# Twenty-five instead of fourteen seven-product pairs in a fused attention and mixer kernel, with a new order of all its tasks

## The chip, the cores and the metric

The kernel runs on one core of one Trainium2 chip. A core has five engines that work side by side, each through its own instructions in a fixed order: PE (TensorE, matrix products, into the eight banks of PSUM), DVE (VectorE), ACT (ScalarE), POOL (GpSimd, here almost only an issuer of DMAs) and SP (SyncE, an issuer of DMAs). They wait for each other by semaphores. The metric is the device time of one execution in microseconds (us); the time of a kernel is the median of its runs.

## The reference

Windowed attention with a distance bias, then a low-rank mixer over the sequence and an MLP with a residual:

```python
B, H, S, D = q.shape                      # 4, 8, 768, 64
scores = scale * np.matmul(q, k.transpose(0, 1, 3, 2))
# keep: the first 8 keys, and the 96 keys up to the query; bias: -slope[h] * distance
a = np.exp(scores - scores.max(-1)) / (sum + 1e-09)
x = (a @ v).transpose(0, 2, 1, 3).reshape(B, S, 512)
xt = x.transpose(0, 2, 1)
h = xt @ U @ V                            # U: 768 x 32, V: 32 x 768
u = x + h.transpose(0, 2, 1)
out = u + np.maximum(u @ w_ch1, 0.0) @ w_ch2   # w_ch1: 512 x 2048, w_ch2: 2048 x 512
```

## The kernel before

**Tasks and their order.** The kernel describes its work as some hundreds of tasks, each with a name, an engine, a function that issues its instructions, the tasks it needs, and the buffers it takes and gives back (`Task`, `Group`, `Planner`). A planner that ran earlier has fixed everything that can vary: `ORDER` is the list of all tasks in issue order, `SLOTS` the buffer or PSUM bank of each group, `CFG` which engine does a task that several could do. `Planner.run` checks that list against the needs, and a loop at the end issues the tasks as listed, so each engine's order is that of `ORDER`.

**The stages, by name.** A number behind the name is the pair (0 to 15: two heads of one batch, four pairs a batch) or batch and part.

- Loads: `lq`, `lk`, `lv` (q, k, v of a pair; POOL, but for pair 0, whose q and k come as fp32 on SP and are cast by `Cq`, `Ck`), `w1_0` to `w1_7` and `w2_0` to `w2_3` (slices of the MLP weights, POOL), `u16` (U), `mixl`, `vs` (V of the mixer).
- Constants: `iota`, `relf`, `rel3` (distances), `bias` (scaled identities in `ib`), `mask` (exponentials of the distances, ACT).
- Attention of a pair: `TK`, `TQ` (transposes on PE for the early pairs, by DMA on SP from pair 8), `EK`, `EQ` (their copies out of PSUM), `KO` and `VC`/`VG` (copies of K and V with the global keys at the front of each block), `SB` (bias by PE, batch 0), `S` (scores), `EX` (exponential, ACT), `MK` (multiplication by the mask, DVE, batches 1 to 3), `PV` (values), `RC`, `NM` (division, DVE), `XC` (copy to fp16).
- Mixer: `UP` transposes x by PE and multiplies it by U. Every pair multiplies with U at 32 columns (`xu` is true, line 752), so that the result lies with tokens on partitions' side; then `XE` copies it out four times over (128 columns), `XU` turns it by one more matmul (line 855), `TE` copies that out as `tmp`, `HM` multiplies by V and adds it to the transposed x, `E0`/`E1` copy the sum out as `uT`, the input of the MLP.
- MLP-1 (u @ w_ch1, 16 column blocks of 128, two halves of the tokens): a plain block is `M1a`.. `M1b` (four matmuls of 384 columns for each half; lines 927 and 951) and a ReLU on ACT (`RL`, `RM`).
- Blocks z and z+8 can be done as a pair with seven products instead of eight (`Z` in `CFG`, line 1022 and after): `ZT` forms four differences of `uT` once a batch, `ZS` four sums of weights, kept in `zs` or formed anew in an `ep` buffer, `ZP1` to `ZP7` are two matmuls of 384 columns each into three PSUM banks, `ZU`, `ZW`, `ZX` copy partial sums to fp32 buffers (ACT, four buffers `zu` in batches 0 to 2), `ZA`, `ZB`, `ZD` add them with the ReLU (a custom DVE instruction, line 1040), `ZR` is the fourth ReLU (ACT). Before, 14 of the 32 pairs are done so: z = 4 to 7 in batches 1 and 2, 2 to 7 in batch 3.
- MLP-2 (h @ w_ch2): always seven products, `P1` to `P7` of eight matmuls of 256 columns each (line 1139), with sums of its operands by DVE (`PA`, `PB`, lines 1092 to 1098; `TWa`, `TWb` once for the weights), a low-rank part by `RS`, additions to the residual by `DA`, `DB`, `DC`, `DD`, `DF`, `DG`, `DH` (lines 1151 and 1191) and stores `O` on SP (line 1206). In the last batch the third part of the tokens is cut into halves (`P43.2a`, `P43.2b`, `DG3.2a`, `DG3.2b`, stores `a`, `b`, `c`).

**What stands around.** MLP-1 and MLP-2 of a batch are interleaved with the attention of the next. Ahead of the first transpose eight matmuls of 512 columns on zeros run (`WARM`, `idle`, line 1240); nothing reads their result.

Of the kernel before, what the change touches and what calls it, by code (L numbers as in the profile page):

```python
# [26 lines left out]
TK5 TE0 RC2 HM0 NM2 lk7 PV3.0 E00 TK4 PV3.1 EK5 XC2 UP1 RC3.0 RC3.1 TQ5 EK4 w1_5 XE1 PV3.2 EQ5 XU1 UP2 NH3.0 w1_6 TQ4
NH3.1 XE2 TE1 RC3.2 XU2 EQ4 lv4 HM1 TE2 NH3.2 HM2 E01 KO4 back UP3.0 mixl w1_2 UP3.1 UP3.2 NM3 M1a0.3 XE3 lv5 E02 XU3
M1c0.3 TE3 mask2 HM3 w1_4 S4.1 E13 E03 M1d0.3 KO5 EX4.1 w1_0 TK7 M1b0.15 EK7 M1a0.2 vs2 lq6 RM0.15 M1b0.3 KO7 EX4.2
M1a0.15 M1c0.2 RL0.3 M1a0.13 RL0.15 S4.0 S5.0 EX4.0 M1d0.2 lq7 M1b0.13 RL0.13 M1b0.11 EX5.0 M1b0.2 mask1 w1_3 M1a0.4  # L30
RL0.2 M1a0.10 w2_2 mask0 RL0.4 S5.1 MK4.2 RM0.13 w2_0 M1a0.12 MK4.1 RM0.11 EX5.2 M1a0.14 VC4 ZS5 M1b0.14 RL0.10 VG4
RL0.14 M1b0.10 VC5 mask5 MK4.0 M1a0.11 EX5.1 lk6 M1a0.0 mask3 M1c0.0 PV4 RM0.10 MK5.2 w2_3 RL0.11 TQ7 RM0.14 RC4
M1b0.5 VG5 RL0.12 w2_1 NM4 M1b0.4 lv7 MK5.1 XC4 M1b0.8 PA0.3 M1d0.0 RM0.8 M1b0.0 M1b0.6 TD0 RL0.0 lq9 MK5.0 M1a0.7
RM0.4 RM0.6 PV5 M1b0.12 RC5 EQ7 M1a0.5 NM5 RM0.12 RM0.5 M1b0.7 RL0.5 TWa0 M1a0.6 RL0.7 mask6 lk9 TK6 RM0.7 M1a0.1
TWb0 EK6 M1c0.1 M1b0.9 M1d0.1 PB0.3 RM0.9 M1b0.1 RL0.6 TQ6 lq8 RL0.1 UP4 EQ6 M1a0.9 KO6 XE4 PA0.0 XU4 M1a0.8 TE4
RL0.9 PA0.1 RS0.0 RL0.8 S7.0 lv8 HM4 P10.0 E04 PA0.2 EX7.0 P20.0 lv6 PB0.0 XC5 S6.1 RS0.1 PB0.1 EX6.2 lk8 P10.1 PB0.2
EX6.1 P20.1 lk11 TWa1 UP5 P30.0 XE5 mask4 TQ8 TWb1 P50.0 lv9 XU5 P30.1 TE5 DA0.0 MK6.1 S6.0 HM5 DA0.1 EX6.0 P60.0
DF0.0 E05 VC6 P60.1 DF0.1 MK6.2 S7.1 TK8 VC7 RS0.2 VG6 EX7.1 P10.2 DB0.1 MK7.0 TK9 EX7.2 P50.1 MK6.0 VG7 MK7.1 P70.1
TQ9 MK7.2 P30.2 VC8 ZS7 PV6 KO8 lk10 DB0.0 PV7 DC0.0 P20.2 DD0.1 DA0.2 lq10 RC7 P70.0 RC6 NM7 P40.1 NM6 XC7 lk12
P60.2 DG0.1 XC6 DF0.2 UP7 KO9 DD0.0 lq11 UP6 DB0.2 XE7 DC0.1 P40.0 XE6 TK10 XU6 XU7 P70.2 lv11 DG0.0 TE6 TE7 VC9 TQ10  # L40
HM6 lv10 HM7 DD0.2 S8.0 E17 ZP11.4 E07 EX8.0 P40.2 ZS4 lq13 E06 S8.1 P50.2 ZT1 EX8.1 ZP11.5 EX8.2 M1a1.3 ZU1.5 lk13
M1b1.3 ZU1.4 ZP61.5 RL1.3 ZP21.5 VG11 ZP61.4 ZA1.5 ZW1.5 S9.1 ZW1.4 DC0.2 M1b1.6 EX9.1 O0.1 ZS6 ZP71.5 ZP71.4 MK8.2
O0.4 ZX1.5 lq12 ZP11.7 EX9.2 O0.2 M1a1.7 DG0.2 TQ11 ZP51.4 RL1.7 ZP41.5 RM1.6 ZP21.4 ZP51.5 ZR1.5 O0.0 M1a1.6 ZB1.5
M1a1.2 ZA1.4 ZX1.4 O0.3 MK9.1 RL1.6 O0.5 ZP21.7 TK11 ZB1.4 M1b1.2 MK8.1 ZP41.4 M1a1.5 VG8 ZR1.4 MK8.0 ZU1.7 ZP31.4
ZP11.6 RL1.2 KO10 ZD1.4 ZP31.5 ZP61.7 ZA1.7 S9.0 ZD1.5 ZW1.7 M1b1.7 EX9.0 TQ12 PA1.2 PV8 RL1.5 ZP21.6 ZU1.6 RC8
ZP51.7 RM1.7 ZP61.6 NM8 ZP71.7 M1b1.5 ZX1.7 ZA1.6 ZW1.6 M1a1.4 RM1.5 MK9.0 KO11 lk14 ZP71.6 ZB1.7 M1a1.0 ZX1.6 PB1.2
# [1237 lines left out]
```

## Time and profile before

| | us |
|---|---|
| median of three runs | 220.88 (220.48 to 221.22) |
| profiled execution, its own time | 220.31 |
| span in the profile, first to last instruction | 218.5 |
| granted TensorE clock | 1.00 of full speed |
| first matmul of MLP-1 starts | 26.90 |
| last matmul of a product starts | 214.50 |
| last store lands | 217.14 |

The page gives for each engine the busy time; the windows give it for a stretch; the chain of waits follows the last work back to what released it; the groups list instructions by line with count, busy time and mean duration. A PE that is busy by the profile is not always at its peak, since the end of a matmul is modelled: the interval between the starts of two that follow each other is the better measure.

### The profile page before, as it was taken

What the parts mean: (1) busy time and instruction counts of PE and PEld (TensorE: products, weight loads), DVE (VectorE), ACT (ScalarE), POOL (GpSimd) and SP (SyncE); (2) the same over time, 40 slices, a digit from 0 to 9 for tenths busy, and PEclk for the clock granted to TensorE, in tenths of its full rate; (3) what the DMA queues carried; (4) which work ended last, traced back from release to release, by engine and by line L of the source; (5) the groups of instructions that cost most, each with busy time, mean ns of one, the idle gap of its engine ahead of it and who ended that gap; (6) DMA issues with size and microseconds to landing.
All of it is one profiled execution on the core that took longest, in us unless ns stands there. A gap on an engine that the chain in (4) does not pass through costs nothing.

```text
span 218.5 us, 5715 instructions
## 1 busy us (share of the span) xinstructions
PE 211.2 (97%) x2320; PEld 152.5 (70%) x2320; DVE 169.2 (77%) x380; ACT 136.5 (62%) x250; POOL 72.9 (33%) x96
## 2 busy tenths in 40 slices
PE   7899999999999999999999999999999999999993
PEld 3466755666879865567788976666889865568882
DVE  4578844879999985989888589769869666789952
ACT  5899999978843589578825376977643347760000
POOL 7988976843824973071106300010000000000000
PEclk9999999999999999999999999999999999999999
DMA  6999999999999999999986986430000004000045
GB/s 167 176 166 145 162 186 177 195 194 184 149 147 129 119 148 170 297 138 120 78 176 49 103 143 207 89 38 2 3 0 3 3 0 163 29 3 0 27 168 194
DMA packets 96618, 25.39 MB, mean 116 GB/s; under 512 B 84016, under 2 KB 94000, under 8 KB 96592
## 3 DMA queue, kind: packets, MB, share of 16 engines
q0 software_dynamic: 72096, 13.54, 78.4%
q1 hardware_dynamic: 24496, 11.49, 24.6%
q8 instruction: 18, 0.29, 0.5%
q14 instruction: 8, 0.07, 0.1%
HBM read 27.56 MB, written 6.29 MB: 155 GB/s over the span
## 4 chain that ended last, share of the span: by engine, by line
PE 68%; DVE 15%; DMA 7%; POOL 3%; issue 3%; ACT 1%; DVEq 0%; POOLq 0%
PE ps L1139 27%; PE ps L1022 14%; PE ps L927 10%; PE ps L951 6%; DMA vt<-in_v_dram 4%; DMA w<-in_moe_w_ch_dram 3%; PE ps L641 3%; DVE x_sb L1151 2%; PE ps L774 2%; PE ps L747 2%; PE ps L773 1%; POOL stgq L356 1%; DVE ep L719 1%; PE ps L1131 1%; PE ps L873 1%
## 5 line engine op out<-in xcount | busy, mean ns | idle before, releaser
L706 ACT ACTIVATE ep<-ps 128x1024 f16<-128x1024 f32 (+1 forms) x48 | 44.0, 955 | 10.6 <-PE ps L641 10.4
L1139 PEld LDWEIGHTS <-htr 128*128 128x128 f16 x392 | 36.3, 98 | 5.7 <-issue 1.1
L927 PE MATMUL ps<-uT,w 128*128 128x384 f16 x176 | 33.1, 326 | 0.4 <-DMA w<-in_moe_w_ch_dram 0.4
L1151 DVE TENSOR_TENSOR x_sb<-x_sb,ps 128x256 f32<-128x256 f32 (+1 forms) x60 | 26.6, 464 | 8.3 <-PE ps L1139 8.1
L1139 PEld LDWEIGHTS <-sA 128*128 128x128 f16 x288 | 27.1, 98 | 4.3 <-issue 1.0
L356 POOL DMA_DIRECT2D stgk<-in_k_dram x24 | 20.2, 851 | 20.9 <-DMA kT<-stgk 18.1
L927 PEld LDWEIGHTS <-w 128*128 128x128 f16 x176 | 16.5, 98 | 11.2 <-DMA w<-in_moe_w_ch_dram 0.8
L1139 PE MATMUL ps<-w,sA 128*128 128x256 f16 x192 | 23.8, 273 | 0.0
L1139 PE MATMUL ps<-tB,htr 128*128 128x256 f16 (+1 forms) x200 | 23.7, 268 | 0.0
L1139 PE MATMUL ps<-w,htr 128*128 128x256 f16 x192 | 23.5, 273 | 0.0
L360 POOL DMA_DIRECT2D vt<-in_v_dram x16 | 16.7, 1050 | 20.1 <-PE ps L641 12.0
L951 PE MATMUL ps<-uT,w 128*128 128x384 f16 x112 | 22.7, 326 | 0.0
L356 POOL DMA_DIRECT2D stgq<-in_q_dram x24 | 20.1, 850 | 6.7 <-DMA w<-in_moe_w_ch_dram 4.1
L933 ACT ACTIVATE htr<-ps 128x384 f16<-128x384 f32 x44 | 19.8, 500 | 3.6 <-PE ps L927 3.3
L1040 DVE CUSTOM_DVE_ANT_0 htr<-ps,zu 128x384 f16<-128x384 f32 x30 | 15.9, 552 | 7.0 <-PE ps L1022 6.4
L719 DVE TENSOR_TENSOR ep<-ep,mask 128x1024 f16<-128x1024 f16 x24 | 15.9, 681 | 4.0 <-ACT mask L1226 3.8
L261 ACT ACTIVATE zu<-ps 128x384 f32<-128x384 f32 x30 | 14.1, 491 | 7.7 <-PE ps L1022 5.1
L812 DVE TENSOR_TENSOR x_sb<-ps,rcp 128x768 f32<-128x768 f32 x16 | 15.1, 952 | 0.3
L951 PEld LDWEIGHTS <-w 128*128 128x128 f16 x112 | 10.5, 98 | 6.6
L1022 PEld LDWEIGHTS <-w 128*128 128x128 f16 x108 | 10.2, 98 | 6.8 <-issue 0.8
L261 ACT ACTIVATE x<-x_sb 128x768 f16<-128x768 f32 x10 | 8.4, 843 | 9.7 <-DVE x_sb L812 9.6
L641 PE MATMUL ps<-qT,kT 64*128 64x128 f16 x192 | 13.9, 217 | 0.5 <-ACT qT L261 0.5
(123 smaller groups left out, 419.0 us busy)
## 6 DMA issues: line engine op xcount, KB each, us to landing
out_dram<-x_sb SPq DMA_DIRECT2D x20, 256.0 KB, 2.4
vt<-in_v_dram POOLq DMA_DIRECT2D x16, 192.0 KB, 6.8
stgk<-in_k_dram POOLq DMA_DIRECT2D x24, 96.0 KB, 5.8
stgq<-in_q_dram POOLq DMA_DIRECT2D x24, 96.0 KB, 5.8
w<-in_moe_w_ch_dram POOLq DMA_DIRECT2D x8, 256.0 KB, 7.6
w<-in_moe_w_ch_dram POOLq DMA_DIRECT2D x4, 512.0 KB, 10.4
out_dram<-x_sb SPq DMA_DIRECT2D x7, 128.0 KB, 2.5
stgq<-in_q_dram POOLq DMA_DIRECT2D x3, 192.0 KB, 5.8
```

The costliest lines, as they stand in the source:

```text
L261: nc.scalar.activation(dst, src, AF.Copy)
L356: nc.gpsimd.dma_start(o[:, i], src[b, h0 + i].rearrange("(n p) d -> p n d", p=P))
L360: nc.gpsimd.dma_start(vt[gv.slot][:, :, :, 0:D], v[b, h0:h0 + 2].rearrange("h (n p) d -> p h n d", p=P),)
L641: nc.tensor.matmul(t[:, hi, j * P:(j + 1) * P], lhs, qt[r, i * P:(i + 1) * P], start=not biased, stop=True, skip_group_check=biased,)
L706: nc.scalar.activation(ep[gep.slot][:, :, lo:512], ps[:, gsc.slot:gsc.slot + 2, lo:512], AF.Exp, scale=qk_scale)
L719: nc.vector.tensor_tensor(ev, ev, mv, ALU.mult)
L927: nc.tensor.matmul(ps[:, g.slot, 0:HS], w1[:, dc, jt * P:(jt + 1) * P], ub[:, dc, i * HS:(i + 1) * HS], start=(dc == 0), stop=(dc == NDC - 1),
L933: nc.scalar.activation(htr[:, jt, i * HS:(i + 1) * HS], ps[:, g.slot, 0:HS], AF.Relu)
L951: nc.tensor.matmul(ps[:, g.slot + half, 0:HS], w1[:, dc, jt * P:(jt + 1) * P], ub[:, dc, half * HS:(half + 1) * HS], start=(dc == flat[0]) ...
L1022: nc.tensor.matmul(bank(g), a()[:, i], bq[:, i], start=first and i == 0, stop=last and i == 1, skip_group_check=True,)
L1139: nc.tensor.matmul(o if part is None else o[:, part], a[:, j, c0 + cols.start:c0 + cols.stop], bq[:, j] if part is None else bq[:, j, part ...
L1151: nc.vector.tensor_tensor(o, o, x, ALU.add)
```

## The change

- `Z` becomes z = 5 in batch 0 and all eight pairs in batches 1 to 3: 25 pairs. All eight weight sums are kept (`ZK` of eight); the room for three of them is a tile `once` that held `ib`, `early` and `rel3`, which are dead by then.
- Pairs 0 to 3 leave `NU`: their U-product runs at 128 columns against `uz`, a copy of U spread by a memset (`uz`) and a fan-out copy (`uc`, DVE), and gives the final layout at once. `XE` and `XU` of these pairs are gone.
- The matmuls on zeros become 24 tasks `w0` to `w23` of the plan, eight of one matmul of 512 columns, sixteen of four of 128 columns.
- The load of pair 0's k and q no longer wait for each other in the plan, and q is first.
- `ORDER`, `SLOTS` and the engine strings of `CFG` are new. Each engine's whole instruction order changes. DVE has 407 rows of instructions instead of 380, ACT 259 instead of 249, PE 2358 matmuls instead of 2320.

```diff
 CFG = {
-    "NU": (0, 1, 2, 3, 4, 5, 6, 7, 8, 9, 10, 11, 12, 13, 14, 15), "back": "EK1", "early": 4, "att1": (0, 1, 2, 3, 4, 5, 6, 7),
+    "WV": 8, "WN": 16, "UC": "D", "NU": (4, 5, 6, 7, 8, 9, 10, 11, 12, 13, 14, 15), "back": "EK1", "early": 4,
...
-    "Z": ((1, (4, 5, 6, 7)), (2, (4, 5, 6, 7)), (3, (2, 3, 4, 5, 6, 7))), "PA": "DDDDDDDDDDDDDDDD", "PB": "DDDDDDDDDDDDDDDD",
-    "ZK": (4, 5, 6, 7), "ZE": {}, "AC": {}, "NZU": 4, "S1": ((0,), (1, 2)), "OS": ((0, 0), (0, 1)),
+    "Z": ((0, (5,)), (1, (0, 1, 2, 3, 4, 5, 6, 7)), (2, (0, 1, 2, 3, 4, 5, 6, 7)), (3, (0, 1, 2, 3, 4, 5, 6, 7))),
+    "PA": "DDDDDDDDDDDDDDDD", "PB": "DDDDDDDDDDDDDDDD", "ZK": (0, 1, 2, 3, 4, 5, 6, 7), "ZE": {}, "AC": {}, "NZU": 4,
...
-    "TE": "DADDAAAAAAAAADAA", "XE": "AAAADAAAADAAAAAA", "EK": "ADADDDADAADDAADD", "EQ": "DAAAAADDADAAAAAA",
-    "KO": "ADDDDDADAASSSAAS", "HR": "RRRRRRRRFRRRFRRR", "IB": "AAAA", "U16": "Q", "VS": "QQD", "C0": "DAADDADA", "DL": (),
-    "SPL": (0,), "BI": (0, 1, 2, 3), "EKS": "AADADADA", "EQS": "ADDADADA", "KOS": "DDDADADA", "VO": "DDDDDDDDDDSSADSD",
-    "XC": "DDADAAAAAADDAAQA", "E": "AAADAAADAADDAAAD",
+    "TE": "DADDAAAAAADDAAAA", "XE": "AAAAAAAAAAAADDAA", "EK": "AAADDDAAAADDAADD", "EQ": "DDDDDDAAADAAAAAA",
+    "KO": "ADADAAAAAAASDSSS", "HR": "RRRRRRRRFRRRFRRR", "IB": "AAAA", "U16": "Q", "VS": "QQD", "C0": "ADDDDADA", "DL": (),
+    "SPL": (0,), "BI": (0, 1, 2, 3), "EKS": "DDDADADA", "EQS": "AADADADA", "KOS": "ADDADADA", "VO": "DDDDDDAASSSSASSS",
+    "XC": "AAADDDAAAAADAAQD", "E": "AAADAAADADADAAAD",
...
-WARM = {
-    "TK0": (8, 512, 7),
-}
...
-    ib = sb("ib", [P, H, P], FP16)
-    early = sb("early", [P, 1024], FP16)
+    once = sb("once", [P, 2304], FP16)
+    ib = once[:, 0:H * P].rearrange("p (h c) -> p h c", h=H)
...
-    zs = sb("zs", [P, len(ZK), 3, 2, P], FP16) if ZK else None
+    zs = [once[:, 768 * i:768 * i + 768].rearrange("p (i a b) -> p i a b", i=3, a=2) for i in range(3)]
+    zs += sb("zs", [P, 3, 2, P], FP16, len(ZK) - 3)
+    uz = zs[-1].rearrange("p i a b -> p (i a) b")
...
-                t = add(SP, 0.5, ldf, sp_loads[-1:], lat=2.6 + 0.55 * len(sp_loads), name=f"l{nm}{p}")
+                t = add(SP, 0.5, ldf, lat=2.6 + 0.55 * len(sp_loads), name=f"l{nm}{p}")
...
+    c_uz = add(DVE, 0.27, lambda: nc.vector.memset(uz, 0.0), name="uz")
+    ue2 = ENG[CFG["UC"]]
+
+    def fan():
+        copy(ue2, uz.rearrange("p n (a g r) -> p n a g r", a=2, g=2)[:, :, :, 0], u16.unsqueeze(2).broadcast_to((P, NB, 2, R)))
+
+    c_uc = add(ue2, {DVE: 0.3, ACT: 0.5}[ue2], fan, [c_u16, c_uz], fast=1, name="uc")
...
                 for c in () if xu else cs:
                     nc.tensor.matmul(
-                        ps[:, gx.slot, 384:512], u16[:, c].rearrange("p g r -> p (g r)"), xx[:, c],
+                        ps[:, gx.slot, 384:512], uz[:, c], xx[:, c],
                         start=False, stop=(c == NB - 1), skip_group_check=True,
                     )
...
+    for i in range(CFG["WV"] + CFG["WN"]):
+        g = Group("ps")
+        n, width = (1, 512) if i < CFG["WV"] else (4, 128)
+        add(
+            PE, 0.2135 if i < CFG["WV"] else 0.222, lambda g=g, n=n, width=width: idle(g, n, width), [c_wz], acq=[g], rel=[g], name=f"w{i}",
+        )
```

What the new `ORDER` has at the places that the prediction speaks of (all engines together, as listed; a `w` is a task on zeros):

```diff
-lk0 wz iota lq1 lq0 relf rel3 lk1 ones3 lk2 vz mask7 bias0 vs1 Ck0.0 bias1 Ck0.1 ones1 ones0 bias2 TK0 lv0 SB0.2
+lq0 ones2 wz vz lk1 w7 lk0 w6 iota w4 lq1 relf w1 uz bias1 rel3 w0 lk3 bias0 w3 ones1 ones0 lv0 Cq0.0 mask2 SB0.1
+mask0 vs0 w5 Cq0.1 bias2 Ck0.1 Ck0.0 TQ0 lq2 bias4 TK0 EQ0.1 SB0.2 EK0.1 lk2 mask3 w2 EK0.0 EQ0.0 lv1 TK1 KO0.1 KO0.0
...
-DC3.1 DB3.2 P33.1 DF3.0 P63.1 DF3.1 P53.0 DB3.1 O3.1 P73.2 O2.3 O2.0 P73.0 DD3.2 P73.1 DD3.0 DC3.2 P43.0 DD3.1 O3.5a
-P33.2 DC3.0 DG3.0 P43.1 O3.0 DH3.2 O3.2 P43.2a DG3.1 O3.3 P43.2b O3.4 DG3.2a DG3.2b O3.5b O3.5c
+P33.0 DD3.2 DB3.0 P33.1 DC3.1 DC3.2 P73.1 DF3.0 O3.5a P43.2a O2.5 DD3.1 P23.1 O2.4 DG3.2a O3.5b P73.0 DF3.1 O2.0 O2.3
+P43.1 O3.1 P43.2b DG3.1 P33.2 DD3.0 O3.4 DG3.2b O3.0 P43.0 DH3.2 O3.5c w21 O3.2 w14 DG3.0 w18 w15 O3.3 w13 w8 w23 w20
+w10 w9 w17 w19 w11 w16 w12
```

On POOL's queue the weight slices of MLP-1 stand as w1_7, w1_1, w1_3, w1_5, w1_4, w1_6, w1_0, w1_2 instead of w1_1, w1_7, w1_5, w1_6, w1_2, w1_4, w1_0, w1_3, still among loads of the pairs 4 to 7.

More of the change, by code (lines that the diff above doesn't have):

```diff
@@ L27 @@
[L27 to L46, printed above, removed]
@@ L435 @@
         c_u16 = add(
-            POOL, 0.84, lambda: nc.gpsimd.dma_start(u16[:, :, 0], moe_U.rearrange("(c p) r -> p c r", p=P)), size=0.35, name="u16",
+            POOL, 0.84, lambda: nc.gpsimd.dma_start(u16, moe_U.rearrange("(c p) r -> p c r", p=P)), size=0.35, name="u16",
         )
```

124 lines of the change are left out of this document (75 added, 49 removed), and 3 rows, old and new, of the table CFG.

## The prediction

> **What bounds the kernel now.** I read four views, in this order: the page's busy times, the windows by stage, the chain of waits, and the groups of instructions.
>
> ```profile
> span 218.5 us, 5715 instructions
> PE 211.2 (97%) x2320; PEld 152.5 (70%) x2320; DVE 169.2 (77%) x380; ACT 136.5 (62%) x250; POOL 72.9 (33%) x96
> PE 68%; DVE 15%; DMA 7%; POOL 3%; issue 3%; ACT 1%; DVEq 0%; POOLq 0%
> ...
> L1040 DVE CUSTOM_DVE_ANT_0 htr<-ps,zu 128x384 f16<-128x384 f32 x30 | 15.9, 552 | 7.0 <-PE ps L1022 6.4
> ```
>
> PE works 97% of the span. DVE (77%) is second; the last line is its cost in the seven-product scheme.
>
> ```profile
> 0.00:27.00 27.00, 24.56 (x374) 15.08 (x375) 18.97 (x57) 23.09 (x37) 24.18 (x40) 1.00 1.66 162
> 27.00:38.60 11.60, 11.10 (x106) 6.32 (x105) 5.24 (x13) 10.54 (x19) 8.11 (x11) 1.00 1.81 182
> 38.60:134.50 95.90, 95.53 (x1077) 71.17 (x1076) 82.16 (x177) 65.20 (x120) 39.79 (x46) 1.00 1.53 152
> ...
> 48.70:59.40 10.70, 10.70 (x126) 7.91 (x124) 10.42 (x21) 9.53 (x18) 6.57 (x9) 1.00 2.01 169
> 59.40:70.10 10.70, 10.70 (x151) 9.08 (x148) 10.48 (x25) 5.25 (x9) 3.92 (x6) 1.00 1.60 142
> ```
>
> The columns are stage, length, then busy time of PE, PEld, DVE, ACT and POOL, granted clock, DMA share, GB/s. There are three regimes. To 27 us (the first MLP-1 matmul starts at 26.90) loads, ACT (23.1 of 27) and DVE set the pace. From 27 us to the last product (its last matmul starts at 214.50) PE sets it: 26.90 to 214.5 is 187.6 us, and the PE tasks in it, each at the interval at which its kind follows itself, sum to 183.4, so only 4.2 us are stalls. Then 4.0 us for the last addition, store and closing waits. The two short windows matter most: there DVE is busy 10.4 of 10.7 us while PE does not stall.
>
> ```profile
> 57.19 0.47 DVE htr L1097
> 57.66 0.47 DVE sA L1098
> 58.13 0.47 DVE htr L1097
> ...
> 182.55 6.66 PE ps L1022 x40
> ```
>
> From the chain (start, us): 768-element DVE operations whose own duration is 551 ns start every 0.47 us, so DVE work is priced by such intervals: 0.47 for L1040's additions too (0.465 to 0.475 back to back). Forty matmuls of 384 columns take 6.66 us, 0.163 to 0.167 each; I use 0.163, what runs of eight in the chain (1.30 us) show.
>
> **The change, part by part.**
>
> *Eleven more seven-product pairs.* A plain pair is 16 matmuls of 384 columns, a seven-product pair 14. PE: 11 x 2 x 0.163 = -3.6 us, all after 27 us, where PE sets the pace. ACT: still four half-size evacuations per pair. DVE: 33 more additions x 0.47 = 15.5 us; one more set of differences of uT, 2.1; eight weight sums instead of six, 2 x 1.17 = 2.3; V copies of six pairs (to SP's queue and ACT) and K copies of three (to ACT) leave, -4.0; two evacuations of K or Q, a half one and a fan-out come, about +3. By these intervals DVE's total goes from 162 to 181 us.
>
> Where this falls decides. Between equal amounts of PE work (93.4 us, with the same 42 eight-matmul products and eight attention pairs), which took 95.9 us above, DVE has 79.3 us of work now. In the changed order, from ZP10.5 to ZP22.3, it has 92.2: 17 more additions (8.0), five more weight sums (5.9), three more masks (1.8), 12 fewer V copies (-2.9), small things. DVE and PE are then equal for 93 us. The trace has no stretch that long with both full, so I bound the wait. Low: 0, as in 48.7 to 70.1, where DVE had 20.5 us of such work in 21.4 and PE none to wait for. High: DVE gets only the share it had over the longer 38.6 to 80.5, 38.0 of 41.9 or 91%: 92.2/0.91 = 101.3, +5.4. I take +1.3 (a share of 95%), near the low end because the dense row is the nearer case and its PE did not stall at all. What waits there: an addition that is late holds its PSUM bank, then the product that reuses the bank, and PE runs in order behind it; ACT's next copy waits for one of four fp32 buffers.
>
> [...]
>
> *U-product of batch 0 in the final layout.* Six 32-column matmuls become 128-column ones. One pair's U matmuls lie 0.025 us before their successors at 32 columns, 0.056 at 128: 6 x 0.031 = 0.19, less the turning matmul that is dropped (0.056): +0.13, for four pairs +0.5 us. All four stand ahead of MLP-1 in both orders, where PE waits for ACT and the loads. Uncovered it is 0.5, covered 0; I take +0.2, since the last of them leads to MLP-1 directly. ACT loses four copies (L261 xus, 0.17 each when back to back: -0.7) before 27 us, and each pair one hop. DVE gets a memset and a fan-out copy, 0.5, covered by DVE's waits (0.5 to 1.7 us idle at five places before 18 us), except that the memset stands ahead of the mask base and delays it by 0.2, which the next part has.
>
> *Start.* Q is loaded before K on SP (landings 3.8 and 5.0 us), iota stands behind a K load on POOL (one issue, 0.83 us), and two masks stand ahead of K's cast on ACT. Adding up ACT's list: mask base at 4.4 instead of 3.2, K cast at 5.7 to 6.1, first exponential at about 9.05 instead of 8.70. From there to the copy that frees MLP-1, ACT has 16.1 us of work against 16.6. Net -0.2.
>
> The first eight idle matmuls run at 0.427 us, and the next 512-column ones at 0.21, so PE runs at half rate to about 4 us.
>
> ```profile
> 0.89 3.42 PE L1240 MATMUL ps<-zero 128*128 128x512 f16 x8 [0.89 <-POOL zero L278]
> ```
>
> Now six stand together (2.6 us), then PE idles about 1 us for the mask base. If the half rate lasts through the next two transposes and biases, K's transpose is 0.6 us later; if not, 0. I take +0.2, so the start costs 0, bounds -0.7 and +0.8. [...]
>
> *Loads.* Now M1a0.13 waits 0.5 us (at 32.17) for the weight slice landing at 32.1. In the new POOL order the first four slices serve eight column blocks (64 matmuls x 0.163 = 10.4 us); by the 1.3 to 1.6 us between landings the fifth and seventh land near 34.5 and 37, before use. -0.4 (0 to -0.5). Later loads shift among neighbours; they share the bound of the next part.
>
> *SP.* The V copies of four more pairs, three DMAs each, go through SP's queue (seven pairs instead of three; K copies stay four), among the transposes that stand there in order: a copy that waits for its V load holds the next transpose, and that the scores of a later pair. Such copies landed 2.4 to 5 us after issue, and PE has MLP work ahead of those scores. Nothing, and up to +1 if one lands late (the range has it).
>
> *End.* Idle matmuls are 8 of 512 columns and 16 tasks of 4 x 128. One of the latter stands in batch 2 (+0.2), 15 after the last product: 15 x 4 x 0.056 = 3.3 us. The last product is a full one, P43.0: its addition takes 0.42 instead of 0.28, its store is 256 KB (2.4 us to land) instead of 64 KB (1.8): +0.7 us after the last addition's start.
>
> ```profile
> out_dram<-x_sb SPq DMA_DIRECT2D x20, 256.0 KB, 2.4
> ...
> out_dram<-x_sb SPq DMA_DIRECT2D x2, 64.0 KB, 1.8
> ```
>
> Both ways the end comes about 4.4 us after PE's last real product instead of 4.0, since the closing waits on SP stand for every engine's work: +0.5 (0.3 to 0.9).
>
> **Sum** against the profiled execution (220.31 us: span 218.5 and 1.8 around it): -3.6 (pairs) + 0.2 (U-product) + 0 (start) - 0.4 (loads) + 0.2 (idle task in batch 2) + 0.5 (end) + 1.3 (DVE) = -1.8, so 218.5. The three timed runs have a median 0.57 higher, 220.88; the forecast is 220.88 - 1.8 = 219.1 us.
>
> **The rivals.** (A) DVE becomes the bound between 40 and 135 us. For: equal work for 93 us, where now it is equal for 21. Against: those 21 us without a stall. The other terms sum to -3.1, so at 91% (+5.4) the time is 223.2 us. It decides once DVE is idle over about 7% of the stretch (99.0 us instead of 95.9, where the 3.1 is gone). (B) Hardly a new stall, and the new order also removes part of the 4.2 us of old ones. For: DVE kept up in the dense windows. Against: three engines are now above 85% there. 220.88 - 3.1 - 1 = 216.8. (C) The start is late: half-rate PE, K last, a queue behind iota. For: ACT and POOL are 86 and 90% busy to 27 us, so nothing is caught up. Against: ACT has 0.5 us less to do. +1.5 on the forecast: 220.6. (D) DVE operations do not overlap in the denser order: 104.5 us of full durations in the stretch instead of 95.9, +8.6, so 226.4. The rows speak against it. [...] That fewer pairs than announced change can't be: the new list holds 175 products, 25 x 7.
>
> **How the numbers follow.** Forecast 0.53 (own range 217.6 to 220.4), A 0.21, B 0.13, C 0.11, D 0.02. A measurement of this kernel tells 0.3%, 0.7 us, from no change (its runs lie 0.74 apart). Faster: 0.46 of the forecast, B and 0.03 of C, 0.62; same: 0.07 of the forecast, 0.03 of A and 0.05 of C, 0.15; slower: the rest of A and C, and D, 0.23. Low 216.3 is B with most of the start's better bound; high 223.0 cuts A just short of its 91%.
>
> **What would show it.** PE's time from first MLP-1 matmul to last product near 184 to 186 us (now 187.6): right. DVE above 95% from 40 to 135 us with PE stalls of 1 to 2 us more: right; PE idle behind L1040's successor for 4 us or more: A. First MLP-1 matmul within 0.7 us of 26.9: the start is right; 512-column matmuls at 0.427 us after 4.5 us: C. The last product followed by 3.3 us of idle matmuls and the end 4.3 to 4.9 us after it: the end is right.

## The result and the profile after

The changed kernel takes 221.68 us (median of 20 runs, 220.43 to 222.92), the kernel before 220.77 (20 runs, 219.89 to 221.86): a ratio of 1.0044, 95% interval 1.0026 to 1.0062. It is slower by about 1 us where 1.8 us less were forecast; the whole interval lies on the slower side. The profiled execution of the changed kernel took 222.24 us, 1.93 more than that of the kernel before, and its span is 1.95 longer; the account below is made between these two spans.

The page of the changed kernel: span, busy times, shares of the chain of waits, and the group of DVE additions.

```profile
span 220.4 us, 5864 instructions
...
PE 214.6 (97%) x2358; PEld 155.3 (70%) x2358; DVE 183.7 (83%) x411; ACT 140.4 (64%) x264; POOL 73.1 (33%) x96
...
PE 81%; DVE 9%; DMA 4%; issue 2%; POOL 1%; ACT 1%; POOLq 0%; DVEq 0%
...
L1055 DVE CUSTOM_DVE_ANT_0 htr<-ps,zu 128x384 f16<-128x384 f32 x59 | 30.8, 552 | 5.0 <-PE ps L1037 3.6
```

(The lines of the changed code lie 13 to 15 further down: the additions are L1055 instead of L1040, the products of MLP-1 L1037 instead of L1022, those of MLP-2 L1154 instead of L1139, the copy of x to fp16 L850 instead of L837. The page counts 411 instructions on DVE and 264 on ACT, a few more than the list of the change has.) The additions have nearly doubled, 16 to 31 us, and DVE works 14.5 us more. PE's share is the same 97%, and its busy time is 3.4 us *more*, though it has fewer products to do: the matmuls on zeros that now stand behind the last product are 3.7 us of it.

```profile
215.78 3.69 PE L1254 MATMUL ps<-zero 128*128 128x128 f16 x60
```

They don't explain that the last product comes 1.2 us later. So the question is in which stretch PE is busy or waiting for longer. The windows of the changed kernel (columns as before: length; busy PE, PEld, DVE, ACT, POOL; granted clock; DMA share; GB/s):

```profile
0.00:27.53 27.53, 25.22 (x366) 15.73 (x367) 19.84 (x57) 23.54 (x39) 24.12 (x39) 1.00 1.61 167
27.53:38.00 10.47, 10.47 (x103) 6.32 (x102) 6.90 (x16) 10.12 (x17) 8.62 (x11) 1.00 1.92 177
38.00:134.50 96.50, 95.83 (x1080) 70.82 (x1079) 91.95 (x204) 70.76 (x136) 39.51 (x47) 1.00 1.52 152
146.00:150.30 4.30, 2.40 (x25) 1.46 (x23) 4.06 (x9) 2.19 (x6) 0.82 (x1) 1.00 0.49 46
150.30:155.30 5.00, 4.96 (x35) 2.61 (x35) 2.61 (x7) 2.66 (x5) 0.00 (x0) 0.66 0.00 0
215.80:220.40 4.60, 3.67 (x62) 3.49 (x59) 0.42 (x1) 0.00 (x0) 0.00 (x0) 1.00 0.68 243
```

From 38 to 134.5 us, the stretch that the forecast feared for, DVE is at 95% and PE hardly waits. The fourth and fifth rows are new: PE works 2.4 of 4.3 us, and then 5 us at a clock of 0.66. What PE waits for stands in its timeline (start, duration, instruction, how many; in brackets the idle time before it and what ended it); below it, its line among the waits of PE (us in total, times, longest).

```profile
147.53 0.81 PE L1037 MATMUL ps<-zt,w 128*128 128x384 f16 x4
148.18 0.22 PE L868 MATMUL ps<-ident,xus 128*128 128x128 f16 x1
150.34 0.23 PE L760 MATMUL ps<-ident,x 128*128 128x128 f16 x1 [1.94 <-DMA x<-x_sb]
...
154.05 1.35 PE L1154 MATMUL ps<-w,htr 128*128 128x256 f16 x8
```

```profile
PE ps L760 <- DMA x<-x_sb: 1.9, 1, 1.9
```

The matmul at 150.34 is the first of UP14, and what it waits for is `XC14`: the copy of pair 14's x to fp16, which `CFG` gives to POOL as a DMA (letter Q in the string `XC`). It is the only one that is made so, in both kernels. The page of the kernel before had its price in the list of DMA issues, and the two timelines of POOL show when it is issued, before and after:

```profile
x<-x_sb POOLq DMA_DIRECT2D x1, 192.0 KB, 3.2
```

```profile
144.67 0.82 POOL L837 DMA_DIRECT2D x<-x_sb  x1 [22.10 <-PE ps L1022]
```

```profile
147.06 0.82 POOL L850 DMA_DIRECT2D x<-x_sb  x1 [21.96 <-PE ps L1037]
```

Before, it is issued at 144.67, lands at 147.92, and UP14 runs at 148.75: 0.8 us of slack, since twelve PE tasks (4.5 us by the plan's own times) stand between `XC14` and `UP14` in `ORDER`. In the new order there are five (ZP72.1, UP12, ZP52.1, ZP42.0, XU12), 1.5 us, and a landing that takes 3.2 us is waited for. Counted from the end of `PV14`, from which XC14's input is worked out, the loss has two parts: PE is ready for UP14 after 4.1 us instead of 6.1, and XC14 is issued after 2.9 us instead of 2.0, since DVE comes to `RC14` later and now has an addition of a seven-product pair between it and `NM14`, whose result XC14 copies.

Behind the wait the clock falls. With half rate for x us, five us at 0.66 mean 5 - x/2 = 3.3, so x is 3.4 us. The window from 151.30 to 154.70 us, which opens 1 us after the end of the gap, shows them: 3.4 us at a granted clock of 0.50. Eight matmuls of 256 columns that begin in it at 154.05 take 1.35 us instead of 1.04. A gap of 1.94 us stood ahead of it. The runs list a granted clock of 0.992 in 14 of 20 executions of this kernel (3.4 us at half rate are 0.8% of the span) and 1.000 in six.

The account, with the stalls counted in one way for all kernels (the interval between the starts of two PE tasks, less what the first needs; a wait inside a task is put down to the one behind it). The prediction's own count for the kernel before had 183.4 of work and 4.2 of stalls in the same 187.6 us, so only the differences are compared.

| | before | after | difference | forecast |
|---|---|---|---|---|
| first matmul of MLP-1 starts | 26.90 | 27.53 | +0.63 | +0.2 |
| PE work from there to the end of the last product | 182.26 | 178.93 | -3.33 | -3.4 |
| stalls in it | 5.34 | 9.32 | +3.98 | +0.9 |
| from there to the end of the span | 3.98 | 4.66 | +0.68 | +0.5 |
| span | 218.49 | 220.44 | +1.95 | -1.8 |

The end of the last product is the start of its last matmul and one interval more: 214.45 in the trace of the kernel before, so 214.50.

### The profile page after: what moved, and what is told of

Its sections match the earlier page's. It is cut to its first block, busy times and chain, and to the rows that moved or that the text cites. A ratio compares the mean times of both kernels' runs of the same rounds, so it can differ in the third digit from the quotient of the medians.

```text
span 220.4 us, 5864 instructions
## 1 busy us (share of the span) xinstructions
PE 214.6 (97%) x2358; PEld 155.3 (70%) x2358; DVE 183.7 (83%) x411; ACT 140.4 (64%) x264; POOL 73.1 (33%) x96
## 4 chain that ended last, share of the span: by engine, by line
PE 81%; DVE 9%; DMA 4%; issue 2%; POOL 1%; ACT 1%; POOLq 0%; DVEq 0%
PE ps L1154 30%; PE ps L1037 24%; PE ps L940 6%; PE ps L654 4%; DMA u<-in_moe_U_dram 3%; PE ps L964 2%; PE ps L760 2%; DVE x_sb L1166 2%; PE ps L787 2%; PE ps L886 2%; PE ps L1254 2%; PE ps L786 2%; PE ps L523 2%; DMA x<-x_sb 1%; PE ps L1146 1%
## 5 line engine op out<-in xcount | busy, mean ns | idle before, releaser
L1154 PEld LDWEIGHTS <-htr 128*128 128x128 f16 x392 | 36.1, 98 | 7.3 <-issue 2.5
L1055 DVE CUSTOM_DVE_ANT_0 htr<-ps,zu 128x384 f16<-128x384 f32 x59 | 30.8, 552 | 5.0 <-PE ps L1037 3.6
L267 ACT ACTIVATE zu<-ps 128x384 f32<-128x384 f32 x59 | 27.8, 492 | 9.5 <-PE ps L1037 6.6
L1154 PEld LDWEIGHTS <-sA 128*128 128x128 f16 x288 | 27.4, 98 | 3.8 <-issue 0.2
L1037 PEld LDWEIGHTS <-w 128*128 128x128 f16 x200 | 19.1, 98 | 12.1
L1154 PE MATMUL ps<-tB,htr 128*128 128x256 f16 (+1 forms) x200 | 24.2, 268 | 0.3 <-DVE x_sb L1206 0.3
L1154 PE MATMUL ps<-w,htr 128*128 128x256 f16 x192 | 24.3, 275 | 0.0
L1154 PE MATMUL ps<-w,sA 128*128 128x256 f16 x192 | 24.1, 273 | 0.0
L1037 PE MATMUL ps<-uT,w 128*128 128x384 f16 x100 | 22.5, 326 | 0.0
L1037 PE MATMUL ps<-zt,w 128*128 128x384 f16 x100 | 22.1, 326 | 0.0
L1037 PE MATMUL ps<-zt,zs 128*128 128x384 f16 x64 | 15.0, 326 | 0.0
L940 PE MATMUL ps<-uT,w 128*128 128x384 f16 x80 | 14.8, 326 | 0.0
L654 PE MATMUL ps<-qT,kT 64*128 64x128 f16 x192 | 14.1, 217 | 0.0
L267 ACT ACTIVATE uT<-ps 128x768 f16<-128x768 f32 (+1 forms) x15 | 10.4, 722 | 5.1 <-PE ps L886 5.0
```

Source lines behind the costliest of these rows:

```text
L267: nc.scalar.activation(dst, src, AF.Copy)
L654: nc.tensor.matmul(t[:, hi, j * P:(j + 1) * P], lhs, qt[r, i * P:(i + 1) * P], start=not biased, stop=True, skip_group_check=biased,)
L940: nc.tensor.matmul(ps[:, g.slot, 0:HS], w1[:, dc, jt * P:(jt + 1) * P], ub[:, dc, i * HS:(i + 1) * HS], start=(dc == 0), stop=(dc == NDC - 1),
L1037: nc.tensor.matmul(bank(g), a()[:, i], bq[:, i], start=first and i == 0, stop=last and i == 1, skip_group_check=True,)
L1055: return lambda: nc.vector._custom_dve(TENSOR_ADD_SAT, out=o, in0=x(), in1=y(), s0=3.0e38, s1=0.0)
L1154: nc.tensor.matmul(o if part is None else o[:, part], a[:, j, c0 + cols.start:c0 + cols.stop], bq[:, j] if part is None else bq[:, j, part ...
```

## The experiments

All times are medians beside runs of the kernel before on the same chip (medians 220.42 to 220.77); the ratio to them, with its 95% interval, is what is compared. "Start" is the first matmul of MLP-1, "stalls" those from there to the last product, "tail" the rest of the span.

| kernel | time, us | ratio to before | start | stalls | tail |
|---|---|---|---|---|---|
| after, as changed | 221.68 | 1.0044 (1.0026 to 1.0062) | 27.53 | 9.32 | 4.66 |
| e1 cast on ACT | 218.88 | 0.9924 (0.9899 to 0.9948) | 28.09 | 5.75 | 5.00 |
| e2 zeros in the wait | 219.91 | 0.9971 (0.9954 to 0.9989) | 27.14 | 6.05 | 3.77 |
| e7 before, cast on ACT | 220.86 | 1.0019 (0.9999 to 1.0039) | 27.01 | 5.71 | 4.04 |
| e3 e1 and an earlier mask base | 217.49 | 0.9871 (0.9843 to 0.9899) | 26.29 | 5.52 | 4.95 |
| e4 e1 without zeros at the end | 219.18 | 0.9928 (0.9903 to 0.9952) | 27.82 | 5.67 | 5.21 |
| e5 e3 without zeros at the end | 218.01 | 0.9882 (0.9859 to 0.9905) | 26.69 | 5.66 | 4.98 |
| e6 UP14 later | 221.93 | 1.0058 (1.0028 to 1.0088) | 27.67 | 8.31 | 4.80 |
| e6b UP14 later, scores spread | 221.87 | 1.0058 (1.0035 to 1.0082) | 27.69 | 8.47 | 5.05 |
| e9 U-product undone | 222.13 | 1.0064 (1.0034 to 1.0094) | 30.70 | 6.89 | 4.70 |
| e8a 8 additions twice | 222.48 | 1.0087 (1.0056 to 1.0119) | 28.07 | 9.59 | 4.97 |
| e8b 17 additions twice | 226.98 | 1.0293 (1.0265 to 1.0322) | 27.85 | 13.79 | 4.81 |
| e11 8 additions short | 218.54 | 0.9915 (0.9890 to 0.9940) | 27.72 | 5.60 | 4.66 |
| e10 eight zeros at the start | 218.56 | 0.9912 (0.9889 to 0.9934) | 26.97 | 5.53 | 5.23 |
| e12 e3 and e10 | 217.85 | 0.9879 (0.9851 to 0.9907) | 26.65 | 5.68 | 5.14 |

In e2 the zeros that fill the wait count as work (1.78 us), not as stall. All but e7 start from the changed kernel, and of these all but e2, e6 and e6b have the cast on ACT as well.

**The cast on ACT (e1).**

```diff
-    "XC": "AAADDDAAAAADAAQD", "E": "AAADAAADADADAAAD",
+    "XC": "AAADDDAAAAADAAAD", "E": "AAADAAADADADAAAD",
```

> The changed kernel with one letter of the plan other: the fp16 copy of pair 14 (XC14) is made by ACT instead of by a POOL DMA from SBUF to SBUF. Theory 1 (the wait of UP14 for that DMA, 1.94 us, and the half PE clock of 3.41 us that follows it, some 1.7 us): both go, about 3.6 us less than the changed kernel, 218 us, ratio to the kernel before 0.987 to 0.990, granted clock 1.00, no PE gap over 0.5 us between 145 and 155 us. Theory 2 (DVE is the bound from 40 to 150 us, and the wait only shows where its lag comes out): the lag comes out at another PE task, time 220.5 to 222, ratio 0.999 to 1.005.

One letter is worth 1.2% against the changed kernel, about 2.6 us, and turns the sign of the change. ACT makes the copy in 0.84 us. The same two windows of e1:

```profile
146.00:150.30 4.30, 4.30 (x48) 3.00 (x47) 4.06 (x9) 4.08 (x10) 0.00 (x0) 1.00 0.00 0
150.30:155.30 5.00, 5.00 (x66) 3.48 (x66) 4.55 (x10) 3.86 (x6) 0.00 (x0) 1.00 0.01 3
```

PE works all of both, 114 matmuls in place of 60, at full clock. The stalls fall by 3.57 us, from 9.32 to 5.75; the start of this execution was 0.56 later and its tail 0.34 longer, so its span is 2.6 shorter. Theory 1 had 3.6 us and a ratio of at most 0.990; in time about a quarter of that is missing; in the profile it went into the later start and the longer tail.

**The same letter in the kernel before (e7).**

```diff
-    "XC": "DDADAAAAAADDAAQA", "E": "AAADAAADAADDAAAD",
+    "XC": "DDADAAAAAADDAAAA", "E": "AAADAAADAADDAAAD",
```

> The kernel before with the same one letter other (XC14 by ACT). In its trace the copy lands 147.92, UP14 starts 148.75 behind other PE work. Theory 1: no change, ratio 0.998 to 1.002. If ACT is the better engine for the copy in any case: ratio 0.990 to 0.996.

No gain: 1.0019, with an interval that reaches 0.9999. So the DMA cast cost nothing where it had its slack; it is the meeting of this cast with the new order that costs.

**Wait and clock apart (e2).** The cast stays with the DMA, and eight of the tasks of four matmuls on zeros, which otherwise run after the last product, stand just ahead of `UP14`:

```diff
-... XE12 ZP42.0 ZB2.0 XU12 UP14 ZB2.1 ...
+... XE12 ZP42.0 ZB2.0 XU12 w8 w9 w10 w11 w12 w13 w14 w15 UP14 ZB2.1 ...
```

> The changed kernel with eight of the sixteen tasks of four matmuls on zeros (1.8 us in all) moved from the end to just ahead of UP14; the DMA copy stays. Theory 1: UP14 starts as late as in the changed kernel (about 150.3 us), but PE is not idle ahead of it, the clock stays at full speed, 1.5 to 1.8 us less after it and up to 0.3 less at the end: 219.7 to 220.2 us, ratio 0.995 to 0.998. If the clock drop has another cause (it comes 1 us after UP14's start, not in the gap): clock 0.99 as before, 221.3 to 221.7 us, ratio 1.003.

The timeline of PE in e2:

```profile
147.88 0.22 PE L868 MATMUL ps<-ident,xus 128*128 128x128 f16 x1
147.94 2.04 PE L1254 MATMUL ps<-zero 128*128 128x128 f16 x32
150.03 0.23 PE L760 MATMUL ps<-ident,x 128*128 128x128 f16 x1
```

UP14 starts as long after XU12 as before (2.15 us instead of 2.16), but PE has something to do, and no matmul behind it runs at half rate: from 146 to 156 us the granted clock is 1.00. From the start to the last product e2 takes 186.75 us, 1.50 less than the changed kernel and 2.07 more than e1: in these profiles the 3.57 us of the cast are some 2.1 of waiting and 1.5 of half clock. The times agree in order (0.9924, 0.9971, 1.0044), but not all of the step from e2 to the changed kernel is the clock: the six executions of the changed kernel with a granted clock of 1.000 have a mean of 221.31 us, the 14 with 0.992 one of 221.86. That is 0.55 us between them, with times from 220.43 to 222.92 among the six, so it is hardly told apart from their scatter; and e2 lies another 1.4 lower (1.2 by the ratios). In the two profiles e2's tail is 0.9 us shorter, and that comes from SP's stores and not from the clock (see e4, below).

**UP14 at another place (e6, e6b).** In e6 `UP14` and what follows from it (XE14 to E014) stand behind the product P22.1, and the scores S13.1 behind P12.0:

```diff
-... XU12 UP14 ZB2.1 ... HM14 P22.1 E014 ZD2.0 ZD2.1 S13.1 ... P22.0 PA2.0 EX13.2 P12.0 S15.1 DA2.0 ...
+... XU12 ZB2.1 ... P22.1 UP14 XE14 ... P22.0 XU14 TE14 PA2.0 P12.0 HM14 E014 S13.1 EX13.1 EX13.2 S15.1 DA2.0 ...
```

> The changed kernel with the cast of pair 14 still made by POOL's DMA, but UP14 (with XE14, XU14, TE14, HM14, E014) behind P22.1 in the order, and the scores S13.1 behind P12.0. Theory (only PE's place in the order is at fault: 1.9 us of waiting and a half-rate clock behind it): UP14 waits 0 to 0.3 us, no 512- or 256-column matmul runs at half rate after it, and the time is 218.9, within 0.6. Rival (the DMA cast costs by itself, by what it holds up on POOL or in the DMA engines): no better than 221.0. Second rival (a wait of 1 to 2 us turns up elsewhere, since S13.1 and its exponentials are later): 219.5 to 220.5 with a new stall at PV13.

The first theory missed. In the profile UP14 waits for nothing and no half-rate matmul follows (granted clock 1.00 from 147 to 167 us), but the time is that of the changed kernel. The waits of PE in e6, in the stretch around it (us in total, times, longest):

```profile
PE ps L654 <- ACT ep L719: 1.0, 2, 0.5
PE ps L654 <- ACT uT L267: 0.7, 1, 0.7
```

L654 is the scores: S13.1 stops in its middle for the copy E014 that frees its second pair of banks, and S15.1 waits twice for the exponentials that empty the two pairs which S13.1 has just filled. So e6b spreads the scores:

```diff
-... P12.0 HM14 E014 S13.1 EX13.1 EX13.2 S15.1 ... P12.1 ... P52.1 PB2.1 RS2.2 S15.0 P12.2 ... S13.0 ... P32.0 ... P62.0 ...
+... P12.0 HM14 E014 ... P12.1 S13.1 EX13.1 EX13.2 PB2.3 P52.1 S15.1 ... P32.0 RS2.2 P12.2 S15.0 ... P62.0 S13.0 ...
```

> As the run before with UP14 behind P22.1 and the cast left to POOL's DMA, but with the scores S13.1, S15.1, S15.0 and S13.0 each a product apart, so that none waits for the exponential that empties its banks. Theory (the place of UP14 in PE's order is at fault, not the DMA cast): UP14 without a wait, the 1.7 us of waits at S13.1 and S15.1 gone, 218.9 to 220.0. Rival (the DMA cast costs by itself): 221 or more. Second rival (the waits turn up elsewhere, since PE has no other work that is ready there): 220 to 221.

It misses again, 221.87 us. The stalls, 8.47 us, are now many small ones: 0.77 at P32.0 (most of it inside S15.1, just ahead), 0.69 at PV13, 0.44 at P72.0, 0.42 at ZP32.1. Two of them in the waits of PE in e6b (us in total, times, longest), neither of which e1 has in this stretch:

```profile
PE ps L787 <- DVE ep L728: 0.5, 1, 0.5
PE ps L654 <- ACT ep L719: 0.5, 1, 0.5
```

Here L654 is the scores waiting for an exponential, L787 the values waiting for a masked one. The readings fit one chain: the copy, UP14, XE14, XU14, TE14, HM14, the copy E014 that frees banks 4 and 5, the scores that need these banks, their exponentials, the values. Moving UP14 back hides the DMA's 3.2 us from UP14 and hands them to whoever needs its banks. The rival's number (221 or more) came out both times, but not its mechanism: behind the cast POOL has no work left here and the DMA engines are at a share of 0.01 or less from 150.3 to 165 us in both, and in the kernel before the cast cost nothing (e7). Two hand-made orders don't prove that none is better; they show that the lateness does not vanish by moving the instruction that waits.

**The start (e3, e10, e12).** PE's timeline of the changed kernel:

```profile
0.94 2.74 PE L1254 MATMUL ps<-zero 128*128 128x512 f16 x6 [0.94 <-POOL zero L284]
4.80 1.01 PE L635 MATMUL ps<-once 128*128 128x512 f16 x2 [1.12 <-DVE once L304]
5.61 0.63 PE L1254 MATMUL ps<-zero 128*128 128x512 f16 x1
6.04 0.84 PE L523 MATMUL ps<-ident,stgq 128*128 128x128 f16 x6
7.04 0.82 PE L523 MATMUL ps<-ident,stgk 128*128 128x128 f16 x6 [0.16 <-ACT stgk L267]
```

Six matmuls on zeros, a wait of 1.1 us for the mask base, and then everything at half rate: six transposes take 0.84 us (0.51 in the kernel before at 4.60). Full rate is back between 8 and 10 us, in e2 already at 4.8: it varies from run to run, and with it the start, 27.14 to 28.09 us over the nine executions with this order up to there. Two remedies were tried on e1. In e3 the mask base comes earlier:

```diff
-lq0 ones2 wz vz lk1 w7 lk0 w6 iota w4 lq1 relf w1 uz bias1 rel3 w0 ...
+lq0 ones2 wz vz iota lk1 w7 lk0 w6 w4 lq1 relf w1 bias1 rel3 uz w0 ...
```

> As the first kernel of this call (XC14 by ACT), and in the order list iota stands ahead of the first K load on POOL and the memset uz behind the mask base on DVE. If the start of the changed kernel costs on the path to MLP-1 (S0.0 at 9.4 instead of 8.2 us, first MLP-1 matmul at 27.5 instead of 26.9): mask base done 1 us earlier (4.2), S0.0 near 8.6, first MLP-1 matmul 26.7 to 27.1, 0.4 to 0.8 us less than the first kernel, ratio 0.984 to 0.987. If loads or ACT's later work cover it: same as the first kernel within 0.2 us.

In e10 PE has eight matmuls on zeros without a gap, as before the change:

```diff
-... w0 ... w3 ... SB0.1 ... w5 ... TQ0 ... TK0 ... SB0.2 ... w2 ... TK1 ...
+... w0 ... w3 ... w5 w2 SB0.1 ... TQ0 ... TK0 ... SB0.2 ... TK1 ...
```

> The changed kernel with the cast on ACT and the idle matmuls w5 and w2 moved ahead of SB0.1, so that PE runs eight of them without a gap (to about 4.3 us) as before the change; nothing else is moved. Theory (the half rate up to 8 to 10 us is due to the short run of idle matmuls): SB0.1 at 4.8 us at full rate, first scores at 9.1 instead of 10.4, first MLP-1 matmul 27.1 instead of 28.1, time 218.0 to 218.4. Rival (the mask base at 4.8 instead of 3.5 us is what counts, whatever PE does): no change, 218.9.

PE's timeline of e10:

```profile
0.94 3.59 PE L1254 MATMUL ps<-zero 128*128 128x512 f16 x8 [0.94 <-POOL zero L284]
4.80 0.59 PE L635 MATMUL ps<-once 128*128 128x512 f16 x2 [0.27 <-DVE once L304]
5.90 0.51 PE L523 MATMUL ps<-ident,stgq 128*128 128x128 f16 x6 [0.51 <-DVE stgq L269]
```

The mask base is as late as it was (4.80), the clock is full, and MLP-1 starts at 26.97, as the theory said. The other profiles agree in the main: with eight in a row (the kernel before, e7, e10, e12) the half rate is over by 5.7 us, though not always with the eight themselves, and with the changed order it lasts beyond 7.5 us in eight of nine. In time e10 is 218.56, a little above what was expected and, against e1's 0.9924, not told apart from it. In e3 the mask base's matmul starts at 3.48, MLP-1 at 26.29, and the time is 217.49: 0.5% below e1. Both together:

> Cast on ACT, iota ahead of K's loads and the memset behind the distances, and the idle matmuls w5 and w2 ahead of SB0.1. Each of the last two alone brought the first MLP-1 matmul from 27.5 to 28.1 us to about 26.3 to 27.0. Theory (they mend the same thing, a start at half rate, so they don't add): 217.3 to 218.0, first MLP-1 matmul 26.3 to 26.7. Rival (they add): 216.7, first MLP-1 matmul 25.7 or earlier.

They don't add: 26.65 and 217.85. The earlier mask base is the larger part in the time, though the intervals of e3 and e10 just overlap.

**The zeros at the end (e4, e5).** The sixteen tasks w8 to w23 are taken out of `ORDER` ("WN": 0).

> The changed kernel with pair 14's cast on ACT, less the sixteen tasks of four 128-column matmuls on zeros (they produce nothing). The prediction's term for the end: they stand for 0.2 us in batch 2 and about 0.4 us at the end, so 218.3 to 218.5 instead of 218.9, and the time from the end of the last product to the end of the span falls from 5.0 to about 4.3 to 4.6. Rival (the last addition, its store and its landing set the end, and the zeros lie beside them): 218.9, the tail unchanged but for the PE time in it.

> Cast on ACT, iota ahead of K's loads and the memset behind the distances, and no 4 x 128 zeros: if the three parts add, 217.49 less what the zeros cost: 216.9 to 217.2. If the zeros are hidden, 217.5.

The rival had it: 0.9928 against 0.9924, 0.9882 against 0.9871, and in e4 a tail of 5.2 us without a single matmul on zeros. The last addition, its store and the landing set the end, and with them SP's queue. The last addition and the group of stores of the changed kernel, then of e2 (stores: shortest, median and longest issue in ns, start of the first and of the last):

```profile
215.98 0.42 DVE L1166 TENSOR_TENSOR x_sb<-x_sb,ps 128x256 f32<-128x256 f32 x1 [0.45 <-PE ps L1154]
L1221 SPq DMA_DIRECT2D out_dram<-x_sb x14: 332/428/1607, 207.3 to 217.1; - x14
```

```profile
214.09 0.42 DVE L1166 TENSOR_TENSOR x_sb<-x_sb,ps 128x256 f32<-128x256 f32 x1 [0.45 <-PE ps L1154]
L1221 SPq DMA_DIRECT2D out_dram<-x_sb x14: 332/408/1270, 205.4 to 214.5; - x14
```

In e2 the last store is issued as its addition ends. In the changed kernel it is issued 0.7 us after that: one store about 5 us earlier took 1.6 us to issue, and those behind it followed each other without a pause. In both kernels the additions lie at the same distance from the last product. Why a single issue takes so long stays open.

**U-product of batch 0 as it was (e9).** Pairs 0 to 3 back in `NU`, with XE and XU right ahead of each TE.

```diff
-... "NU": (4, 5, 6, 7, 8, 9, 10, 11, 12, 13, 14, 15), ...
+... "NU": (0, 1, 2, 3, 4, 5, 6, 7, 8, 9, 10, 11, 12, 13, 14, 15), ...
```

> The changed kernel with the cast on ACT and the U-product of pairs 0 to 3 undone (32 columns, XE and XU back, right ahead of each TE). The prediction had the new form at +0.2 (0 to 0.5) of PE time, with four ACT copies and a hop fewer: by it the time is 218.7 to 219.1, no change that can be told, and the first MLP-1 matmul moves less than 0.3 us. Rival (ahead of MLP-1 the ACT copies and the hop set the pace): the first MLP-1 matmul 0.7 us or more later, time 219.5 to 219.9.

Both expectations were far too low: MLP-1 starts 2.6 us later than in e1, and the time is 222.13. PE's waits there, and two windows with the clock behind the waits:

```profile
PE ps L869 <- ACT xus L268: 1.3, 3, 0.7
...
PE ps L887 <- ACT tmp L268: 0.4, 1, 0.4
```

```profile
25.00:30.00 5.00, 3.51 (x51) 2.43 (x51) 3.02 (x12) 3.92 (x11) 5.00 (x7) 1.00 1.82 191
30.30:33.80 3.50, 3.48 (x25) 1.71 (x26) 2.95 (x6) 1.83 (x3) 2.40 (x3) 0.52 2.00 173
```

L869 is XU, waiting for its XE on ACT; L887 is HM, waiting for TE. With PE busy for only 3.5 of the 5 us, in gaps of at most 0.7 us, the clock falls here too: to 0.52 of full speed over 3.5 us, just as MLP-1 starts. Six of the nine executions list a granted clock of 0.992. So the time holds a stretch at half clock besides the later start. But the kernel before has these hops too and starts MLP-1 at 26.90; its order was made for them. So this says what the edit is worth to the new order, not what it is worth by itself.

**DVE's load (e8a, e8b, e11).** The addition ZA is issued twice, with the same result, or (e11) over 32 columns only, which leaves out part of the hidden layer. The first edit:

```diff
-return lambda: nc.vector._custom_dve(TENSOR_ADD_SAT, out=o, in0=x(), in1=y(), s0=3.0e38, s1=0.0)
+return lambda: [nc.vector._custom_dve(TENSOR_ADD_SAT, out=o, in0=x(), in1=y(), s0=3.0e38, s1=0.0) for _ in range(n)][-1]
```

> The changed kernel with the cast on ACT and eight of the additions ZA (z odd, batches 1 and 2) issued twice, the second writing the same values: 8 x 0.47 = 3.8 us more DVE work, seven of them between 38 and 134.5 us, where DVE is busy 91.95 of 96.5 us. Theory (DVE still has room there): 0 to 1 us more than 218.9, 218.9 to 219.9. Rival A of the prediction (DVE already sets the pace at about 91 to 95%): every us of DVE comes back as time, 222.2 to 222.7.

> The same with all 17 additions ZA of batches 0 to 2 twice: 17 x 0.47 = 8.0 us more DVE work, sixteen in the stretch, so about 99.5 us of it for 96.5 us. Theory (DVE can be used to nearly 100% before it sets the pace): 3 to 4.5 us more, 222 to 223.4. Rival A (DVE sets the pace already): 8 us more, 226.9. A third outcome, below 221, would say that DVE has more room than its busy time shows.

Rival A's numbers came out, to a tenth: 222.48 where it had 222.2 to 222.7, 226.98 where it had 226.9. From start to last product PE takes 3.84 and 8.05 us more than in e1, for 3.8 and 8.0 us of DVE work. The windows from 40 to 130 us, of e1, e8a and e8b:

```profile
40.00:130.00 90.00, 89.34 (x1019) 66.25 (x1017) 85.98 (x190) 65.28 (x123) 37.65 (x44) 1.00 1.60 146
```

```profile
40.00:130.00 90.00, 88.17 (x994) 65.24 (x992) 86.13 (x189) 63.53 (x120) 39.56 (x47) 1.00 1.58 149
```

```profile
40.00:130.00 90.00, 86.29 (x967) 63.45 (x965) 86.28 (x188) 62.32 (x118) 37.92 (x44) 1.00 1.43 143
```

DVE's busy time (after PE's and PEld's) does not move, 86.0 to 86.3 of 90 (95.5 to 95.9%), while PE's falls from 89.3 to 86.3: about 95.7% is all that DVE reaches over these 90 us, and PE gives way. (A single stretch of 10 us reaches 9.97; in others DVE waits, at much the same places in all three.) That leaves two readings of the changed kernel itself: DVE bounds it, or both are just full.

> The changed kernel with the cast on ACT and the same eight additions ZA (z odd, batches 1 and 2) over 32 columns instead of 384: 352 columns of each are left out, so part of the hidden layer is not written anew. DVE has about 8 x 0.35 = 2.8 us less. Adding 3.8 us of DVE work made the time longer by just as much, with DVE at 95.6 to 95.9% from 40 to 130 us in all three. Theory (PE and DVE are balanced at this number of pairs: PE sets the pace as soon as DVE has room): 0 to 1 us less than 218.9, so 217.9 to 218.9, the DVE share falls to about 93% and PE's work is the same. Rival (DVE alone sets the pace, as rival A has it): 2.8 us less, 216.1.

The window of e11:

```profile
40.00:130.00 90.00, 89.35 (x1018) 66.47 (x1017) 84.66 (x189) 65.20 (x125) 38.23 (x45) 1.00 1.57 148
```

DVE falls to 94.1%, PE's figure stays, and start to last product is 184.54 us against 184.68: balanced. Twenty-five pairs sit on the corner; less DVE work brings nothing, more costs its full length. The waits of PE for DVE say the same. From ZP10.5 to ZP22.3 they are, in the changed kernel, and line for line in e1 and e11:

```profile
PE ps L1154 <- DVE x_sb L1206: 0.3, 1, 0.3
PE ps L654 <- DVE x_sb L1166: 0.2, 1, 0.2
```

Both are additions to the residual. Only with the added work does a product of a pair wait for an addition of a pair, in e8b:

```profile
PE ps L1037 <- DVE htr L1055: 1.1, 3, 0.5
```

## Why the prediction was wrong

**The step that failed: the wait for the copy XC14 is missing from the sum.** The sum has no line for `XC14`. The paragraph on SP prices its V copies and says that one which lands late would cost up to 1 us; the one on loads says that later loads shift among neighbours. The single DMA on POOL whose result PE waits for within the same stage was neither named nor priced. It cost 3.57 us of PE's time in the profile, where forecast and span lie 3.75 apart, and by e1 1.2% of the time, 2.6 us, where forecast and medians lie 2.7 apart. All that was needed lay in the page of the kernel before (3.2 us to land), in its trace (0.8 us of slack) and in the two orders (4.5 us of PE work between the copy and its reader, then 1.5): a wait of about 1.7 us could have been worked out (it was 1.94). The half clock behind it, some 1.5 us in the profile, stands in no row of the kernel before.

With the cast on ACT the time comes near the forecast, 0.9924 or 1.7 us less where 1.8 were forecast. In part that is luck: in the profile of e1 the start (+1.2) and the end (+1.0) are dearer than forecast (+0.2 and +0.5), the stalls (+0.4) cheaper than the +0.9, and that execution is the slowest of its six.

**PE's work.** Eleven pairs less two matmuls each, and one idle task: -3.4 forecast, -3.33 by the matmuls in the trace, each kind at its interval. Right. The sign that the prediction named, 184 to 186 us from the first matmul of MLP-1 to the last product, failed all the same: 188.25, because of the stalls.

**DVE.** Forecast +1.3 between 0 and +5.4, at a share of 95%. The stretch from ZP10.5 to ZP22.3 takes 96.8 us instead of 95.9: +0.9, and the share was 95%, as forecast. But the mechanism of the forecast, a product that waits for the bank which a late addition holds, isn't in the changed kernel's list of waits for that stretch, which goes down to 0.2 us; it comes with the work added in e8a and e8b. And with 2.8 us of DVE work less (e11) the same stretch still takes 96.8 us. So the +0.9 isn't due to DVE's load; what in the new order makes it stays open, and that it nearly meets the forecast is luck. DVE's busy time over the span rose by 14.5 us, in the window of the long stretch from 82.16 to 91.95 us, where the prediction's intervals gave 19 and 12.9. Rival A, DVE as the bound, described the slope on the far side of the corner, and with its 91% put the corner too early. That starts follow each other in less than a duration held as well: the additions kept their 0.55 us, and the time of e8b followed 0.47 for each. Rival D's 104.5 us of durations are in the changed kernel's trace, its lack of overlap isn't: the 204 instructions of DVE from 38 to 134.5 us last 104.6 us added up, in 96.5 us; four additions in a row, from 86.28 us, are done after 1.95 us, 0.47 us from start to start, where their own durations make 2.21.

**Loads.** The wait of M1a0.13, 0.53 us, is gone: -0.5 against -0.4. Together with the stretch's +0.9 and the cast's 3.57 it makes up the stalls' +3.98 (0.04 is left).

**Start and U-product.** Forecast +0.2 with bounds from -0.7; measured +0.63, and 27.14 to 28.09 us over nine executions. The first exponential came at 10.18 us instead of the 9.05 worked out. Rival C's mechanism was there, with 512-column matmuls 0.4 us apart after 4.5 us, at less than its price of 1.5. Its two parts are the late mask base (POOL's issue ahead of `iota`, the memset ahead of `rel3`) and the gap in the idle matmuls; the first was told as a delay of ACT, when its dearer effect was the 1.1 us in which PE stood still, with half rate before and behind. How much each part has isn't settled: the intervals of e3, e10 and e12 overlap.

**End.** Forecast +0.5 (0.3 to 0.9), measured +0.68, with 3.7 us of matmuls on zeros beside it. The size was right, and e4 shows that the zeros don't set it. Of its mechanism the dearer last store is there: it lands 2.2 us after issue instead of 1.7. But 0.4 us more come from SP's queue, which issues that store 0.7 us after its addition instead of 0.3; the prediction has no such term, and the closing waits, 0.2 shorter, and an addition that starts a little sooner make up for part of it.
